# Two transformer layers on one core: three edits to layer norms and weight copies at the seams of a TensorE-bound kernel

## The chip, the core and the metric

The kernel runs on one core of a Trainium2 chip. A core has five engines with instruction streams of their own: TensorE (PE, matrix products), VectorE (DVE), ScalarE (ACT), GpSimd (POOL) and SyncE (SP, which here only issues transfers), and 16 DMA engines that all queues share. The metric is the device time of one launch in microseconds (us), lower is better. A time is the median of several runs; the profile describes one further run.

## The reference

The input x has 2048 tokens of 512 features, in fp32. There are 32 heads of 16 features, and a hidden layer of 1792.

```python
def _layernorm(x, axis=-1, eps=1e-5):
    m = jnp.mean(x, axis=axis, keepdims=True)
    v = jnp.var(x, axis=axis, keepdims=True)
    return (x - m) / jnp.sqrt(v + eps)

def _A_ref(x, wqkv, wo):            # q, k, v = x @ wqkv, 32 heads of 16
    scores = jnp.einsum("bhqd,bhkd->bhqk", q, k) * (Dh ** -0.5)
    p = _softmax(scores, axis=-1)
    o = jnp.einsum("bhqk,bhkd->bhqd", p, v)
    return o.reshape(B, S, D) @ wo

def _B_ref(x, w1, b1, w2):          # Dense, Mish, Dense
    h = x @ w1 + b1
    sp = jnp.log1p(jnp.exp(-jnp.abs(h))) + jnp.where(h > 0, h, 0)
    return (h * jnp.tanh(sp)) @ w2

x = A_x
x = x + _A_ref(_layernorm(x), A_wqkv, A_wo)
x = x + _B_ref(_layernorm(x), B_w1, B_b1, B_w2)
x = x + _A_ref(_layernorm(x), A_wqkv, A_wo)
x = x + _B_ref(_layernorm(x), B_w1, B_b1, B_w2)
```

Both layers use the same weights.

## The kernel before

**Precision.** TensorE works on fp32r operands, a shorter form of fp32. Each fp32 operand is therefore split into a high part (a rounded copy) and a low part (the operand less its high part), and a product takes three matmuls: high x high, high x low, low x high (`mm3`, L196). What PE computes in PSUM is split on the way out by `split_psum` (L192): ACT writes the high part, then DVE the low part.

**Stages.** The 2048 tokens go in four chunks of 512 (`NCH`); a chunk has four token tiles of 128 tokens. Per layer: a layer norm of each chunk gives `th` and `tl`, the high and low parts of the normed chunk turned over (features on the partitions); `qkv` makes the projections of Q and K, each a tile `qk` of 128 features x 512 tokens in PSUM, emptied into a `pt` tile and stored to DRAM (`scr<-pt`), from where `ks` and `qs` are gathered by heads; then come the V phase, the attention, the output projection with residual, a second norm and the hidden layer with residual.

**Order.** PE's order is written down by hand: each matmul is chained to the one before (`att.pe`). `behind` pins the order of other instructions to the order of the program text; what isn't pinned is placed by the framework's scheduler, which decides by its own estimate of time before the kernel is built. Tiles come from pools of a fixed number of buffers (`blk`: 22 large ones; `tmp` with the tags `raw`, 3 buffers, and `f` and `ah`, 2 each); a new tile waits for the last reader of the tile whose buffer it takes.

**The first norm** (`norm_parts` with the tag `mx`) makes statistics of a token tile on DVE (`bn_stats`, `bn_aggr`), the reciprocal root on POOL (`rstd`, L209), and the scaled tile `xn` on DVE (L218). PE then transposes two token tiles into one PSUM tile `tp` of two banks (L248), and one `split_psum` empties both. Between these steps PE runs a few matmuls on a tile of zeros (`warm_up`). The first two weights, `sqkv0` and `sqkv2`, are loaded and split beside it by `split_load`: the high part on ACT (L153), the low part (L156) on DVE for `sqkv0` and on POOL for `sqkv2`.

**The V phase** (`v_parts`) makes the projection of V. For every two token tiles POOL clears a tile `v` (L628), PE makes the product, ACT empties it into `v` (L642), and SP stores it to DRAM (`vscr<-v`, L646). Twelve of the sixteen token tiles are done at the end of `qkv`, the last chunk inside the attention's start.

**The weights kept.** Layer 1 uses the split weights of layer 0 again. `keep` (L142) copies a split weight to DRAM by a DMA of POOL's queue. The six of QKV are copied by `keep_all` at attention step 3, after the last clearing of `v`.

**Layer 1's last norm** (`norm_units(..., wide=True)`, `late` in the layer loop) works on the last chunk of layer 0's output, which is ready last. It is a sequence of steps that `qkv` takes between its projections: four of statistics, four of scaling plus a 32x32 block transpose on DVE (`xn` to `y`), stores of `y` to DRAM (`ntq<-yq`, L308, two sets of four on SP's queue), a load back in turned order (L317), and the rounding (L320, L321). The list in the layer loop says ahead of which projection each step stands:

```python
order = [(0, 0), (0, 1), (4, 0), (4, 1), (1, 0), (0, 2), (4, 2), (1, 1), (1, 2), (5, 0), ...]
for n in (0, 0, 0, 0, 1, 1, 2, 2, 2, 9, 10):
    within.setdefault((n, 0), []).append(lambda: next(late))
```

A pair in `order` is (block of 128 features, chunk). Every second projection (even number) puts its `pt` into the `raw` ring, the others into `blk` buffers.

Of the kernel before, what the change touches and what calls it, by code (L numbers as in the profile page):

```python
# [9 lines left out]
F32 = mybir.dt.float32  # L10
# [8 lines left out]
P = 128  # L19
# [21 lines left out]
AHEAD = 21  # L41
PRE = 3
KEEP = 3
PREP = 2
WARM = (4, 1, 1)
GSTEPS = NCH * NKT
# [32 lines left out]
def kernel(ctx: ExitStack, tc: tile.TileContext, x, wqkv, wo, w1, b1, w2, out):  # L79
# [25 lines left out]
    def b8(shape, dt, name):  # L105
        return blk.tile(shape, dt, tag="blk", name=name)
# [21 lines left out]
    def behind(ins):  # L128
        return tc.keep_in_program_order(ins)
# [73 lines left out]
    def norm_parts(src, nm, got, key, tag, fine=False, pin=lambda ins: ins, pe=lambda ins: ins, halves=False):  # L203
        st = tmp.tile([P, NCH, 6], F32, tag="st", name=f"st{nm}")
        mv = tmp.tile([P, NCH, 2], F32, tag="mv", name=f"mv{nm}")
        ve = tmp.tile([P, NCH], F32, tag="ve", name=f"ve{nm}")
        rs = tmp.tile([P, NCH], F32, tag="rs", name=f"rs{nm}")

        def rstd(t, n):  # L209
            nc.gpsimd.tensor_scalar(ve[:, t : t + n], mv[:, t : t + n, 1], EPS, None, op0=ALU.add)  # L210
            nc.gpsimd.tensor_tensor(rs[:, t : t + n], ve[:, t : t + n], mhalf[:, t : t + n], op=ALU.pow)

        xns = []

        def scaled(t, tag):
            xn = t512(tag, f"xn{nm}{t}")
            pin(
                nc.vector.tensor_scalar(  # L218
                    xn, src[:, t], mv[:, t, 0:1], rs[:, t : t + 1], op0=ALU.subtract, op1=ALU.mult
                )  # L220
            )
            return xn

        def next_scaled():
            xns.append(scaled(len(xns), ("f", "ah")[len(xns) // 2]))

        for t in range(NCH):
            pin(nc.vector.bn_stats(st[:, t], src[:, t]))
            pin(nc.vector.bn_aggr(mv[:, t], st[:, t]))
            if fine:  # L230
                rstd(t, 1)
                if t and tag == "mx":
                    next_scaled()
        if not fine:
            rstd(0, NCH)
        yield
        th = b8([P, KT, CW], F32R, f"th{nm}")
        tl = b8([P, KT, CW], F32R, f"tl{nm}")
        got[key] = (th, tl)
        if tag == "mx":  # L240
            while len(xns) < NCH:
                next_scaled()
            yield
            for u in range(NCH // 2):
                tp = ps.tile([P, 2, 512], F32, tag=tag, name=f"tp{nm}{u}")
                for e in range(2):
                    for k in range(KT):
                        pe(nc.tensor.transpose(tp[:, e, ts(k, P)], xns[2 * u + e][:, ts(k, P)], ident))  # L248
                two = ts(u, 2 * P)
                split_psum(  # L250
                    th[:, :, two].rearrange("p k (t n) -> p k t n", n=P),
                    tl[:, :, two].rearrange("p k (t n) -> p k t n", n=P),
                    tp.rearrange("p t (k n) -> p k t n", n=P),
                    pin,
                )
                yield
            return
        for t in range(NCH):
            xn = scaled(t, "f")
            if halves:  # L260
                yield
            tp = pbank(tag, f"tp{nm}{t}")
            for k in range(KT):
                pe(nc.tensor.transpose(tp[:, ts(k, P)], xn[:, ts(k, P)], ident))
            split_psum(th[:, :, ts(t, P)], tl[:, :, ts(t, P)], tp.rearrange("p (k n) -> p k n", k=KT), pin)
            yield
# [7 lines left out]
    def norm_units(src, nm, got, key, wide=False):  # L274

        st = tmp.tile([P, NCH, 6], F32, tag="st", name=f"st{nm}")
        mv = tmp.tile([P, NCH, 2], F32, tag="mv", name=f"mv{nm}")
        ve = tmp.tile([P, NCH], F32, tag="ve", name=f"ve{nm}")
        rs = tmp.tile([P, NCH], F32, tag="rs", name=f"rs{nm}")
        for t in range(NCH):  # L280
            behind(nc.vector.bn_stats(st[:, t], src[:, t]))
            behind(nc.vector.bn_aggr(mv[:, t], st[:, t]))
            if t == NCH - 1:
                nc.gpsimd.tensor_scalar(ve, mv[:, :, 1], EPS, None, op0=ALU.add)
                nc.gpsimd.tensor_tensor(rs, ve, mhalf, op=ALU.pow)
            yield
        turned = dram.tile([D, CW], F32, name=f"nt{nm}")
        for h in range(2):
            if wide and h == 0:
                xns = b8([P, 2, 2, D], F32, f"xn{nm}")  # L290
                ys = b8([P, 2, D // TR, 2, TR], F32, f"y{nm}")
            if wide:
                xn, y = xns[:, h], ys[:, h]
            else:
                xn = tmp.tile([P, 2, D], F32, tag="raw", name=f"xn{nm}{h}", bufs=3)
                y = tmp.tile([P, D // TR, 2, TR], F32, tag="raw", name=f"y{nm}{h}", bufs=3)
            for j in range(2):
                t = h + 2 * j
                behind(
                    nc.vector.tensor_scalar(  # L300
                        xn[:, j], src[:, t], mv[:, t, 0:1], rs[:, t : t + 1], op0=ALU.subtract, op1=ALU.mult
                    )
                )
                behind(nc.vector.transpose(y[:, :, j], xn[:, j].rearrange("p (b r) -> p b r", r=TR)))
                if j:
                    for a in range(P // TR):
                        n0 = h * CW // 2 + a * 2 * TR
                        nc.sync.dma_start(  # L308
                            turned[:, n0 : n0 + 2 * TR].rearrange("(b q) n -> q b n", q=TR),
                            y[ts(a, TR)].rearrange("q b j r -> q b (j r)"),  # L310
                        )
                yield
        th = b8([P, KT, CW], F32R, f"th{nm}")
        tl = b8([P, KT, CW], F32R, f"tl{nm}")
        got[key] = (th, tl)
        raw = tl.bitcast(F32)
        nc.sync.dma_start(raw, turned.rearrange("(k p) n -> p k n", p=P))  # L317
        yield
        for k in range(KT):
            behind(nc.scalar.activation(th[:, k], raw[:, k], AF.Copy))  # L320
            behind(nc.vector.tensor_tensor(tl[:, k], raw[:, k], th[:, k].bitcast(F32), op=ALU.subtract))  # L321
            if k % 2:
                yield
# [6 lines left out]
    class Attention:  # L330
# [10 lines left out]
        def pe(self, ins):  # L341
            if self.chained:
                if self.last is not None:
                    follow(ins, self.last)
                self.last = ins
# [213 lines left out]
    def qkv(l, att, wts, tt, order, within, due):  # L559
# [57 lines left out]
        for c in range(NCH - 1):  # L617
            for _ in v_parts(l, c, wts, tt, att, False):
                i += 1
                if i % 3 == 0:  # L620
                    some_max()

# [197 lines left out]
            keep(*unkept.pop(0))  # L820

    xc = [load_x(0)]
    load_qkv(0, wts, (0,), splits, nc.vector)
    load_qkv(0, wts, (2,), splits)
    xc += [load_x(c) for c in range(1, NCH)]
    nc.sync.dma_start(b1t, b1.rearrange("(f p) -> p f", p=P))
    att = attention(0)
    att.chained = True
    norms = [norm_parts(xc[c], f"q0{c}", tt, c, "mx", True, behind, att.pe) for c in range(NCH)]
    warm = b8([P, CW], F32, "warm")  # L830
    nc.vector.memset(warm, 0.0)

# [4 lines left out]

    warm_up(0, WARM[0])
    next(norms[0])
    splits.pop(0)()  # L840
    next(norms[0])
    next(norms[0])
    warm_up(1, WARM[1])
    splits.pop(0)()
    next(norms[0])
# [2 lines left out]
    for l in range(2):  # L848
        due, within = {}, {}
        if l == 0:  # L850
            order = [(m, c) for c in range(NCH) for m in (0, 4, 1, 5)[: (4, 4, 3, 2)[c]]]
            due[4, 0] = [lambda: load_qkv(0, wts, (1, 3), splits)]
            due[4, 2] = [lambda: load_qkv(0, wts, (4, 5), later)]
            due[0, 3] = [lambda: split_all(splits)]
            due[5, 2] = [lambda: split_all(later)]
            for c, spots in enumerate((((0, 0), (0, 0), (2, 2), (3, 1)), ((3, 2), (3, 2), (6, 1), (6, 3)), ((6, 3), (6, 3), (9, 1), (9, 3))), 1):
                for at in spots:
                    within.setdefault(at, []).append(lambda c=c: next(norms[c]))
        else:
            order = [(0, 0), (0, 1), (4, 0), (4, 1), (1, 0), (0, 2), (4, 2), (1, 1), (1, 2), (5, 0), (5, 1), (5, 2), (0, 3), (4, 3)]  # L860
            att = attention(1)
            att.chained = True
            late = norm_units(x2s[NCH - 1], f"q1{NCH - 1}", tt, NCH - 1, True)
            for n in (0, 0, 0, 0, 1, 1, 2, 2, 2, 9, 10):
                within.setdefault((n, 0), []).append(lambda: next(late))
        order += [(m, c) for m in (1, 5, 2, 6, 3, 7) for c in range(NCH) if (m, c) not in order]
        qkv(l, att, wts, tt, order, within, due)
# [133 lines left out]
```

## Time and profile before

| what | value |
|---|---|
| median of 3 runs | 3491.2 us (3490.45 to 3491.69) |
| profiled execution, its own time | 3490.85 us |
| its span, first to last instruction | 3489.1 us |
| PE busy | 3475.0 us |
| DVE, ACT, POOL busy | 3004.8, 2576.3, 238.0 us |
| mean granted TensorE clock | 1.000 |

Rows of a timeline show the start, the duration, the engine, the line of the kernel, the operation, what it writes and reads, and how many instructions were put together; in brackets stands the idle time of the engine before it and what ended that. Names are those of the kernel's tiles with numbers left out (`thq`, `tlq`, `xnq` are `th`, `tl`, `xn` of the QKV norms). PE's rows with `x4` are matmuls in a row; their times overlap, since matmuls are pipelined. `SPq`, `POOLq` and `ACTq` are the engines' queues that issue transfers; their duration is that of issuing, not of the transfer.

### The profile page before, as it was taken

To read this page: it belongs to the slowest core of one execution; us is meant where nothing else is said; L and a number is where in the kernel's file an instruction comes from. 1 tells how busy PE (TensorE), PEld (TensorE's weight loads), DVE (VectorE), ACT (ScalarE), POOL (GpSimd) and SP (SyncE) were. 2 spreads that over 40 slices of the span, in tenths; PEclk is the share of its full clock that TensorE was granted. 3 is DMA by queue.
4 is the path that set the end of the run, shared out by engine and by line. 5 is a ranking of instruction groups with operands and counts; after the bars stand their busy time and mean duration, and the time that the engine had idled before them with its cause. 6 is when DMAs were issued, how large, how long until landed. Compare 5 with 4: busy or idle time off the path is not lost.

```text
span 3489.1 us, 68659 instructions
## 1 busy us (share of the span) xinstructions
PE 3475.0 (100%) x28556; PEld 1923.1 (55%) x28556; DVE 3004.8 (86%) x3178; ACT 2576.3 (74%) x3517; POOL 238.0 (7%) x384
## 2 busy tenths in 40 slices
PE   9999999999999999999999999999999999999999
PEld 7644444444444444888876444444444444448887
DVE  6699999999999996767756999999999999957675
ACT  3288888888888889456622888888888888884565
POOL 3100010001001002100010000000000000021000
PEclk9999999999999999999999999999999999999999
DMA  7741313222131314722375202111120212156210
GB/s 246 234 93 43 64 60 75 50 53 72 51 63 56 65 36 96 229 67 73 109 242 158 45 21 58 32 38 34 33 48 21 50 29 48 21 114 213 76 37 25
DMA packets 190019, 277.09 MB, mean 79 GB/s; under 512 B 76356, under 2 KB 118276, under 8 KB 175884
## 3 DMA queue, kind: packets, MB, share of 16 engines
q1 hardware_dynamic: 162788, 196.05, 22.8%
q10 hardware_dynamic: 19176, 43.06, 3.6%
q0 software_dynamic: 7744, 33.60, 3.3%
q8 instruction: 224, 3.67, 0.5%
q14 instruction: 87, 0.71, 0.1%
HBM read 159.92 MB, written 111.67 MB: 78 GB/s over the span
## 4 chain that ended last, share of the span: by engine, by line
PE 97%; DVE 1%; ACT 1%; issue 0%; DMA 0%; POOL 0%; DVEq 0%; SPq 0%; ACTq 0%; POOLq 0%
PE pv L484 30%; PE pm L406 18%; PE ss L468 13%; PE sp L458 9%; PE h L747 9%; PE mo L773 8%; PE qk L199 2%; PE qk L200 1%; PE qk L201 1%; PE wo L199 1%; PE wo L201 1%; PE wo L200 1%; PE va L199 1%; PE va L201 1%; PE va L200 1%
## 5 line engine op out<-in xcount | busy, mean ns | idle before, releaser
L410 DVE TENSOR_REDUCE mxv<-pm 128x2 f32<-128x1024 f32 x2048 | 2385.6, 1219 | 144.6 <-PE pm L406 93.9
L459 ACT ACTIVATE p<-sp 128x1024 f32<-128x1024 f32 x1366 | 1395.6, 1022 | 6.6 <-PE ss L468 1.3
L484 PE MATMUL pv<-p,va 128*32 128x256 f32 (+2 forms) x16032 | 1165.7, 392 | 0.5 <-ACT ot L508 0.5
L406 PE MATMUL pm<-ks,qs 48*128 48x512 f32 x4096 | 1101.2, 447 | 0.5
L469 ACT ACTIVATE p<-ss 128x512 f32<-128x512 f32 x1364 | 814.6, 597 | 332.1 <-PE ss L468 255.0
L458 PE MATMUL sp<-qs,ks 50*128 50x512 f32 x2732 | 737.8, 444 | 1.1 <-ACT p L459 1.1
L484 PEld LDWEIGHTS pv<-p,va 128*32 128x32 f32 x16032 | 368.9, 109 | 502.2 <-issue 423.1
L406 PEld LDWEIGHTS pm<-ks,qs 48*128 48x128 f32 x4096 | 453.3, 184 | 346.1 <-issue 186.3
L468 PE MATMUL ss<-qs,ks 50*128 50x512 f32 x1364 | 611.4, 448 | 0.5 <-ACT v L642 0.5
L468 PEld LDWEIGHTS ss<-qs,ks 50*128 50x128 f32 x1364 | 252.4, 185 | 325.8 <-ACT p L469 234.7
L458 PEld LDWEIGHTS sp<-qs,ks 50*128 50x128 f32 x2732 | 268.1, 183 | 186.2 <-ACT p L459 109.1
L427 POOL CAST hi<-nt 128x32 fp32r<-128x32 f32 x64 | 13.3, 208 | 2246.7 <-DVE nt L423 2246.7
L750 ACT ACTIVATE hb<-h,b1t 128x512 f32<-128x512 f32 x112 | 77.1, 689 | 100.0 <-PE h L747 99.2
L754 ACT ACTIVATE hr<-he 128x512 f32<-128x512 f32 x112 | 70.8, 632 | 104.7 <-DVE he L753 104.0
L193 ACT ACTIVATE pt<-qk 128x512 fp32r<-128x512 f32 x64 | 37.8, 596 | 140.9 <-PE qk L201 107.2
L751 DVE TENSOR_SCALAR he<-hb 128x512 f32<-128x512 f32 x112 | 47.6, 425 | 80.5 <-ACT hb L750 74.5
L757 DVE TENSOR_TENSOR hb<-hb,hr 128x512 f32<-128x512 f32 x112 | 77.5, 692 | 45.0 <-ACT hr L755 42.9
L761 DVE TENSOR_TENSOR al<-hb,ah 128x512 fp32r<-128x512 f32 x112 | 77.4, 691 | 28.8 <-ACT ah L760 23.1
L760 ACT ACTIVATE ah<-hb 128x512 fp32r<-128x512 f32 x112 | 70.2, 627 | 29.9 <-DVE hb L757 29.9
L753 DVE SCALAR_TENSOR_TENSOR he<-he 128x512 f32<-128x512 f32 x112 | 76.8, 685 | 17.2 <-ACT he L752 17.2
L755 ACT ACTIVATE hr<-hr,lnhalf 128x512 f32<-128x512 f32 x112 | 81.1, 724 | 3.6
L752 ACT ACTIVATE he<-he 128x512 f32<-128x512 f32 x112 | 70.4, 629 | 17.9 <-DVE he L751 17.9
(224 smaller groups left out, 2976.7 us busy)
## 6 DMA issues: line engine op xcount, KB each, us to landing
scr<-pt ACTq DMA_DIRECT2D x64, 512.0 KB
qs<-scr SPq DMA_DIRECT2D x174, 128.0 KB
ks<-scr SPq DMA_DIRECT2D x174, 128.0 KB
vscr<-v SPq DMA_DIRECT2D x32, 512.0 KB
va<-vscr SPq DMA_DIRECT2D x64, 256.0 KB
oscr<-ot SPq DMA_DIRECT2D x64, 256.0 KB
ww<-sw POOLq DMA_DIRECT2D x14, 1024.0 KB, 4.3
num<-oscr SPq DMA_DIRECT2D x64, 128.0 KB
```

The source lines that it names most:

```text
L199: pe(nc.tensor.matmul(acc, ah, bh, start=first and i == 0, stop=False))
L200: pe(nc.tensor.matmul(acc, ah, bl, start=False, stop=False))
L201: pe(nc.tensor.matmul(acc, al, bh, start=False, stop=last and i == n - 1))
L406: nc.tensor.matmul(pm[:, e], qs[u][rows, q0 : q0 + P], ks[u][rows, ts(n, 512)], start=True, stop=True)
L410: nc.vector.tensor_reduce(self.mxs[b][:, 2 * u : 2 * u + 2, qt, n], pm, axis=AX.X, op=ALU.max)
L458: self.pe(nc.tensor.matmul(sp[:, e], k, q, start=True, stop=True))
L459: nc.scalar.activation(self.pts[-1][:, 0:n], sp[:, 0:n], AF.Exp, scale=SCALE)
L468: self.pe(nc.tensor.matmul(sp, k, q, start=True, stop=True))
L469: nc.scalar.activation(self.pts[i // 3][:, 2], sp, AF.Exp, scale=SCALE)
L484: nc.tensor.matmul(self.accs[b][ts(h, VW), cols], self.va[b // NCH][:, kt, h, :], self.pts[j][:, e, cols], start=kt == 0 and q0 == 0, stop ...
L747: pe(nc.tensor.matmul(acc, w[:, part, k, ts(f % 2, P)], t[:, k, :], start=i == 0, stop=i == 3 * KT - 1))
L773: nc.tensor.matmul(obs[c][t // 2][:, t % 2], act[:, ts(t, P)], w[:, part, f % 2], start=f == part == 0 and act is ah, stop=f == FT - 1 and ...
```

## The change

Three edits.

A, the start. For the first chunk, each token tile is split by itself as soon as PE has transposed it (four ACT and four DVE instructions on 128x512 in place of two each on 128x1024), still in one PSUM tile for two. For all four chunks, the first scaled tile comes after the second tile's statistics, the second and third after the fourth's. The low part of `sqkv0` moves from DVE to POOL, and the weights' splits go one step later in ACT's order.

B, the V phase of layer 0. Four of the six QKV weights are copied to DRAM at four steps of the V phase; the last two stay where all six were.

C, layer 1's last norm. `xn` lies in `tmp` tiles of tags `f` and `ah`, `y` in the `raw` ring, which takes two `blk` buffers less; and its steps are spread over more projections.

```diff
+KEPT = (4, 12, 20, 28)
@@ norm_parts
             if fine:
                 rstd(t, 1)
-                if t and tag == "mx":
+                for _ in range((0, 1, 0, 2)[t]):
                     next_scaled()
@@
                 for e in range(2):
+                    t = 2 * u + e
                     for k in range(KT):
-                        pe(nc.tensor.transpose(tp[:, e, ts(k, P)], xns[2 * u + e][:, ts(k, P)], ident))
+                        pe(nc.tensor.transpose(tp[:, e, ts(k, P)], xns[t][:, ts(k, P)], ident))
+                    if halves:
+                        split_psum(
+                            th[:, :, ts(t, P)], tl[:, :, ts(t, P)], tp[:, e].rearrange("p (k n) -> p k n", n=P), pin
+                        )
+                if halves:
+                    yield
+                    continue
@@ norm_units
-            if wide and h == 0:
-                xns = b8([P, 2, 2, D], F32, f"xn{nm}")
-                ys = b8([P, 2, D // TR, 2, TR], F32, f"y{nm}")
             if wide:
-                xn, y = xns[:, h], ys[:, h]
+                xn = [t512(("f", "ah")[h], f"xn{nm}{h}{j}") for j in range(2)]
             else:
-                xn = tmp.tile([P, 2, D], F32, tag="raw", name=f"xn{nm}{h}", bufs=3)
-                y = tmp.tile([P, D // TR, 2, TR], F32, tag="raw", name=f"y{nm}{h}", bufs=3)
+                pair = tmp.tile([P, 2, D], F32, tag="raw", name=f"xn{nm}{h}", bufs=3)
+                xn = [pair[:, j] for j in range(2)]
+            y = tmp.tile([P, D // TR, 2, TR], F32, tag="raw", name=f"y{nm}{h}", bufs=3)
@@ qkv, V phase
             for _ in v_parts(l, c, wts, tt, att, False):
                 i += 1
+                if l == 0 and i in KEPT:
+                    keep(*unkept.pop(0))
@@ start
-    load_qkv(0, wts, (0,), splits, nc.vector)
-    load_qkv(0, wts, (2,), splits)
+    load_qkv(0, wts, (0, 2), splits)
...
-    norms = [norm_parts(xc[c], f"q0{c}", tt, c, "mx", True, behind, att.pe) for c in range(NCH)]
+    norms = [norm_parts(xc[c], f"q0{c}", tt, c, "mx", True, behind, att.pe, c == 0) for c in range(NCH)]
...
     next(norms[0])
-    splits.pop(0)()
     next(norms[0])
     next(norms[0])
+    splits.pop(0)()
     warm_up(1, WARM[1])
@@ layer loop
-            for n in (0, 0, 0, 0, 1, 1, 2, 2, 2, 9, 10):
+            for n in (0, 0, 1, 1, 2, 2, 3, 4, 5, 9, 10):
                 within.setdefault((n, 0), []).append(lambda: next(late))
```

More of the change, by code (lines that the diff above doesn't have):

```diff
@@ L300, in norm_units @@
                     nc.vector.tensor_scalar(
-                        xn[:, j], src[:, t], mv[:, t, 0:1], rs[:, t : t + 1], op0=ALU.subtract, op1=ALU.mult
+                        xn[j], src[:, t], mv[:, t, 0:1], rs[:, t : t + 1], op0=ALU.subtract, op1=ALU.mult
                     )
                 )
-                behind(nc.vector.transpose(y[:, :, j], xn[:, j].rearrange("p (b r) -> p b r", r=TR)))
+                behind(nc.vector.transpose(y[:, :, j], xn[j].rearrange("p (b r) -> p b r", r=TR)))
                 if j:
```

## Prediction, made before the changed kernel was run

> **What bounds the kernel now.** The page was read first: the engines' shares, then the chain that ended last.
>
> ```profile
> span 3489.1 us, 68659 instructions
> ...
> PE 3475.0 (100%) x28556; PEld 1923.1 (55%) x28556; DVE 3004.8 (86%) x3178; ACT 2576.3 (74%) x3517; POOL 238.0 (7%) x384
> ...
> PE 97%; DVE 1%; ACT 1%; issue 0%; DMA 0%; POOL 0%; DVEq 0%; SPq 0%; ACTq 0%; POOLq 0%
> ```
>
> TensorE is busy for 3475.0 of 3489.1 us, and 97% of the last chain is its own matmuls. The change leaves its list of matmuls as it is, in number and order. So the most that any edit could bring is the 14.1 us in which PE isn't busy, and the time moves only by how long PE stands still near the three edited places. The second view is PE's list of waits (total us, times, longest):
>
> ```profile
> PE qk L199 <- DVE pt L194: 2.9, 2, 1.4
> ...
> PE sp L458 <- ACT p L459: 1.1, 1, 1.1
> PE tpq L248 <- DVE xnq L218: 1.0, 3, 0.7
> ```
>
> These are the three places: the two waits of the projections are at layer 1's last norm, the one of `sp` stands right behind the V phase of layer 0, and the `tpq` waits lie in the first norm. The profiled execution took 3490.85 us, 1.75 outside its span and 0.35 under the median of 3491.2; I sum against 3490.85 and add 0.35 at the end.
>
> **Part A, the start.** Timeline of the first 27 us, by engine (start, duration, engine, line, operation; in brackets the idle time before it and what ended it). PE:
>
> ```profile
> 6.83 0.60 PE L248 MATMUL tpq<-ident,xnq 128*128 128x128 f32 x4
> ...
> 8.10 1.02 PE L836 MATMUL warm<-warm 128*128 128x512 f32 x2
> ...
> 12.00 2.21 PE L589 MATMUL qk<-thq,sqkv 128*128 128x512 f32 x8 [0.25 <-ACT thq L193]
> ...
> 15.18 1.07 PE L589 MATMUL qk<-thq,sqkv 128*128 128x512 f32 x4
> ...
> 17.00 1.07 PE L589 MATMUL qk<-thq,sqkv 128*128 128x512 f32 x4
> ...
> 26.02 0.50 PE L200 MATMUL qk<-tlq,sqkv 128*128 128x512 f32 x1 [0.49 <-DVE tlq L194]
> ```
>
> DVE, ACT and POOL:
>
> ```profile
> 9.63 0.54 DVE L218 TENSOR_SCALAR xnq<-x,mvq,rsq 128x512 f32<-128x512 f32 x1 [0.76 <-POOL rsq L211]
> 10.61 1.23 DVE L194 TENSOR_TENSOR tlq<-tpq,thq 128x1024 fp32r<-128x1024 f32 x1 [0.43 <-ACT thq L193]
> ...
> 16.01 0.69 DVE L194 TENSOR_TENSOR pt<-qk,pt 128x512 fp32r<-128x512 f32 x1 [0.31 <-ACT pt L193]
> ```
>
> ```profile
> 8.60 1.06 ACT L153 ACTIVATE sqkv<-rqkv 128x1024 fp32r<-128x1024 f32 x1 [6.60 <-DMA rqkv<-in_A_wqkv_dram]
> ...
> 15.38 0.60 ACT L193 ACTIVATE pt<-qk 128x512 fp32r<-128x512 f32 x1 [2.49 <-PE qk L589]
> ```
>
> ```profile
> 12.97 2.39 POOL L156 TENSOR_TENSOR sqkv<-rqkv,sqkv 128x1024 fp32r<-128x1024 f32 x1 [3.38 <-ACT sqkv L153]
> ```
>
> Before, PE turns two token tiles into one PSUM tile of two banks, ACT writes the high part of both at once and DVE the low part of both at once. Afterwards each token tile is rounded by itself, but both still lie in the same PSUM tile, and the built program lets PE's transposes of the second token tile wait for DVE's low part of the first. So what ran side by side becomes a chain: transpose, high, low, next transpose. And DVE's order is fixed: the low part of tile 0 stands behind all four scalings, the last of which waited for POOL's `rsq` at 9.63 in the row above.
>
> Lay it out with these rows. The last scaling ended at 9.63 + 0.54 = 10.17; in the new order the statistics of the last tile come up to 0.5 earlier (one scaling of about that length no longer stands before them), but POOL needs its time, so I take 9.9. Low part of tile 0: 0.69 (the 128x512 row at 16.01), to 10.6. Transposes of tile 1: 0.60, to 11.2. High part of tile 1 on ACT: 0.60 (row at 15.38), to 11.85 with the hand-over. ACT then does the high part of the weights, 1.06, to 12.9; meanwhile PE does its warm-up (two rows, 1.02) and the transposes of tile 2. High part of tile 2 to 13.5, low to 14.2, transposes of tile 3 to 14.8, its high part to 15.4. The first projection starts there, at 15.45 in place of 12.00. It is then shorter: it had pauses inside (12.00 to 15.18 until the next projection starts, 3.18), and now runs through in 12 x (17.00 − 15.18)/8 = 2.73. The second projection starts at 18.2 in place of 15.18: +3.0.
>
> Of that a part comes back, since what waits for DVE later has had more time: the 0.49 at 26.02. Against it stand the following chunks' statistics, which now end before their second scaling and deliver that later, taken as 0.3, half of one DVE pass over 128x512 (0.69). The weights' low part that leaves DVE for POOL (2.39 there) ends at 12.9 + 2.4 = 15.3, just before PE needs it at 15.45 + 0.9, and costs nothing; if ACT were a microsecond later, it would cost that microsecond. Part A: +3.0 − 0.5 + 0.3 = **+2.8**, between +2.0 (more comes back) and +3.5 (nothing does, and each of eight hand-overs is 0.05 longer).
>
> **Part B, four weights kept in the V phase.** The issue queues, SP and POOL, and what DMA moved (windows: length, busy time of the five engines, granted clock, DMA share, GB/s):
>
> ```profile
> 152.36 18.93 SPq L646 DMA_DIRECT2D vscr<-v  x4
> ```
>
> ```profile
> 153.52 3.21 POOL L144 DMA_DIRECT2D wqkv<-sqkv  x6
> ```
>
> ```profile
> 80.00:100.00 20.00, 20.00 (x90) 13.73 (x91) 16.31 (x17) 3.59 (x6) 3.37 (x2) 1.00 0.73 211
> 100.00:125.00 25.00, 24.89 (x111) 16.70 (x109) 20.75 (x21) 3.97 (x7) 3.62 (x2) 1.00 0.64 215
> ...
> 150.00:175.00 25.00, 24.60 (x105) 17.50 (x104) 3.90 (x4) 9.33 (x14) 4.97 (x7) 1.00 0.97 358
> ```
>
> PE behind it, in layer 0 and at the same places of layer 1, which keeps no weights:
>
> ```profile
> 181.82 0.85 PE L484 MATMUL pv<-p,va 128*32 128x384 f32 x8
> ...
> 184.43 0.50 PE L458 MATMUL sp<-qs,ks 50*128 50x512 f32 x2 [1.08 <-ACT p L459]
> ```
>
> ```profile
> 1398.99 0.50 PE L199 MATMUL wo<-wo0l,oh 128*128 128x512 f32 x1
> ```
>
> ```profile
> 1916.81 0.85 PE L484 MATMUL pv<-p,va 128*32 128x384 f32 x8
> ```
>
> ```profile
> 3133.10 0.50 PE L199 MATMUL wo<-wo0l,oh 128*128 128x512 f32 x1
> ```
>
> Six copies of 1 MB are issued together at 153.52 and fill the DMA engines (0.97 busy, 358 GB/s) while SP stores V; its four stores there take 18.93 us to issue. ACT's exponentials write to a buffer that such a store must free, and PE loses 1.08 at 184.43. Is this loss recovered later in the attention? From the `pv` at 181.82 to the output projection at 1398.99 are 1217.17 us; in layer 1, 1916.81 to 3133.10 are 1216.29. Layer 0 is 0.88 longer, so most of the 1.08 stays. With two copies left behind the last memset, a third of the backlog is there, and the stall should go: **−1.0**, at best −1.4 (the 0.4 that PE lacks in the window of 150 to 175), at worst 0 (the store waits for something else).
>
> The four moved copies now run beside the gathers of K and Q, between about 80 and 125. At 369 GB/s (358 / 0.97) one takes 2.84 us of all the engines, four 11.4; the free share there is 20 x 0.27 + 25 x 0.36 = 14.4 us. They fit, spaced by some 14 us each. I count nothing for it; where the cover is gone, the rival below has the price. POOL issues each behind a memset that it did anyway, and the next memset is ten microseconds away.
>
> The Trainium skill (DMA: Bandwidth & Descriptors, Queues, rings and completion order) says that a DMA engine takes turns between the queues that have work, packet by packet. By that a lone copy would slow a gather and not stop it, which leaves the sum at nothing too; the row at 152.36 neither proves nor contradicts it.
>
> **Part C, layer 1's last norm.** PE and DVE, then SP's queue:
>
> ```profile
> 1765.48 0.50 PE L199 MATMUL qk<-thq,qkv0l 128*128 128x512 f32 x1 [1.45 <-DVE pt L194]
> ...
> 1778.08 0.50 PE L199 MATMUL qk<-thq,qkv2l 128*128 128x512 f32 x1 [1.41 <-DVE pt L194]
> ```
>
> ```profile
> 1763.10 0.55 DVE L300 TENSOR_SCALAR xnq<-x,mvq,rsq 128x512 f32<-128x512 f32 x1 [1.47 <-POOL rsq L285]
> ...
> 1764.74 0.68 DVE L194 TENSOR_TENSOR pt<-qk,pt 128x512 fp32r<-128x512 f32 x1
> ```
>
> ```profile
> 1729.63 2.13 SPq L308 DMA_DIRECT2D ntq<-yq  x4
> 1733.81 0.38 SPq L317 DMA_DIRECT2D tlq<-ntq  x1
> ...
> 1767.12 6.45 SPq L308 DMA_DIRECT2D ntq<-yq  x8
> ```
>
> At 1765.48 PE needs a PSUM bank that DVE empties with the `pt` of 1764.74; DVE did this late, behind norm steps that waited 1.47 for POOL. In the new order this emptying stands before the norm, and the stall goes, with a small pause behind it: −1.6. The second stall (1.41) hangs on the emptying of a later projection: it stays or goes with what follows. What the change adds: `y` now lies in the ring of three `raw` buffers that the projections' `pt` tiles also use. So the `pt` of the seventh projection must wait until all four `ntq<-yq` stores of the first half have landed. The quiet case: four stores and the load that waits for them are issued from 1729.63 to 1733.81, so the stores had landed 4.2 us after the first issue. Eight stores beside other traffic took 6.45 merely to issue. The first half of `y` is ready at about 1765.7; ACT and DVE then need 0.60 + 0.69 and 0.1 of hand-over, and the ninth projection wants its bank at about 1772.1 (three projections of 2.73 behind 1765.48 less 1.6). With 4.2 the bank is free at 1771.3, and nothing is lost; with 6.5 at 1773.6, and 1.5 is lost. Queued behind that wait is ACT's order: the later `pt` and the late rounding. Part C lies between −1.8 and +0.8 (the first loss comes back entirely and one more wait is late by 0.8); I take the middle, nearer to the quiet row, **−0.9**.
>
> **The sum.** +2.8 − 1.0 − 0.9 = +0.9 on 3490.85 gives 3491.75, as a median 3492.1.
>
> **The rivals.** *The first norm costs little*: DVE's low part of tile 0 finds its place between the scalings, and the chain hides behind the loads. Then A is +0.5, with B and C −1.9, in all −1.4: 3489.8. For it speaks that the tiles' parts are half as long; against it, that DVE's order is fixed. Chance 0.13.
>
> *The late norm waits*: the stores take the busy latency, C is +0.8, the total +2.6: 3493.8. For it: eight stores in 6.45. Against it: they are now spread over more projections. Chance 0.2.
>
> *The clock falls* (slower). The new chain leaves PE idle from about 7.4 to 10.6, where the longest wait of the first norm is 0.7 now (the list of waits). What a cold PE costs shows in the warm-up tile (durations min/median/max in ns):
>
> ```profile
> L836 PE MATMUL warm<-warm x12: 592/596/1219, 1.4 to 11.2; 128*128 128x512 f32 x12
> ```
>
> The first ones take 1219, the later ones 592. The Trainium skill (TensorE: Matmul & The Clock Gate, Part 1: The HAM clock gate) says that PE goes back to half its clock after an idle window of about 3.4 us. The trace shows no idle time of that length after the start; 1.45 did not do it. From the rows: if 3.2 us of idle time decides it, the transposes (3 x 0.6), one warm-up pair (0.5 of it on the path) and some 6 to 10 projection matmuls at 0.23 double, +3.5; with the rest +4.4: 3495.6. Below an idle time of about three microseconds it doesn't occur. Chance 0.14.
>
> *The copies hold up the gathers* (slower by most). If each of the four stops the gathers for its 2.84 and PE has no slack there, up to 11.4 less what is covered, some +7 to +12: from 3498. Against it: 20.00 of 20.00 and 24.89 of 25.00 busy in these windows, with DMA at 0.73 and 0.64. It decides once the gathers' slack is under about 3 us. Chance 0.08.
>
> **How the numbers follow.** My forecast has the remaining 0.45, with 3490.0 to 3494.0 as its own range. A measurement of this kernel can tell about 0.2%, 7.0 us, from no change; nearly all cases lie within it. Slower by more: the copies, and a little for a longer cold stretch, 0.11. Faster by more would need half of all of PE's idle time: 0.03. Within: 0.86. The range from 3488.5 to 3496.5 leaves out the copies and the tails of both sides.
>
> **What would show it.** Right: the first projection (`qk`, two sets of eight) starts at about 15.4, with transposes that wait for DVE `tlq`; `wqkv<-sqkv` in five or so separate rows on POOL from 80 on, and no wait of `sp` on ACT near 184; no wait at the sixth projection near 1765. Wrong: a first projection before 13; a PE clock under 1 behind 10; `ks` or `qs` waits between 80 and 125; a median outside the range.

## The result: slower by 6 us, and the profile after

The changed kernel took 3497.6 us (median of 18 runs, 3495.41 to 3499.45), the kernel before 3491.3 (15 runs beside them, 3490.43 to 3492.92). The ratio is 1.0017, 95% interval 1.001 to 1.0025: 6 us slower. The forecast was 3492.1 with a range to 3496.5, so it missed by 5.5 us, on the slow side; within 0.2%, which had 0.86, it is only just. All medians are over the runs whose granted clock was near full speed (0.997 or more where it is on record, at least 5 runs of a kernel); the other runs, some 20 us and more longer, are all of kernels without part B's edit, the kernel before among them (three of its 18 here), and the profiled run of the second kernel with a changed order is one of them.

The profiled execution took 3497.56, 6.7 us more than that of before. The page of the changed kernel, and its list of waits of PE (total, times, longest):

```profile
span 3495.7 us, 68666 instructions
...
PE 3476.4 (99%) x28556; PEld 1921.6 (55%) x28556; DVE 3002.9 (86%) x3179; ACT 2576.6 (74%) x3519; POOL 239.3 (7%) x385
```

```profile
PE qk L200 <- DVE pt L195: 5.1, 2, 3.7
PE tpq L250 <- DVE tlq L195: 4.1, 2, 2.6
...
PE sp L465 <- ACT v L651: 0.7, 1, 0.7
```

PE has the same 28556 matmuls. The wait of `sp` on ACT's `p` is gone, the transposes now wait 4.1 for DVE, and the projections wait 5.1 in place of 2.9, once 3.7 at a stretch.

Where the time changed is read from PE's timeline: since PE's order is unchanged, any matmul can be laid beside itself. The changed kernel at the places that the prediction shows of before, and one more:

```profile
29.32 0.50 PE L201 MATMUL qk<-tlq,sqkv 128*128 128x512 f32 x1 [0.47 <-DVE tlq L195]
```

```profile
1401.00 0.50 PE L200 MATMUL wo<-wo0l,oh 128*128 128x512 f32 x1
```

```profile
1778.72 0.50 PE L200 MATMUL qk<-thq,qkv2l 128*128 128x512 f32 x1 [1.41 <-DVE pt L195]
...
1790.85 0.50 PE L200 MATMUL qk<-thq,qkv0l 128*128 128x512 f32 x1 [3.67 <-DVE pt L195]
...
1795.29 0.40 PE L200 MATMUL qk<-thq,qkv2l 128*128 128x512 f32 x1
```

```profile
3139.20 0.50 PE L200 MATMUL wo<-wo0l,oh 128*128 128x512 f32 x1
```

and the thirteenth and fourteenth projection in the kernel before:

```profile
1786.37 0.40 PE L199 MATMUL qk<-thq,qkv0l 128*128 128x512 f32 x1
...
1789.32 0.39 PE L199 MATMUL qk<-thq,qkv2l 128*128 128x512 f32 x1
```

| place | before | after | how much later |
|---|---|---|---|
| first chunk's end (26 us) | 26.02 | 29.32 | +3.30 |
| output projection, layer 0 | 1398.99 | 1401.00 | +2.01 |
| tenth projection, layer 1 | 1778.08 | 1778.72 | +0.64 |
| thirteenth projection, layer 1 | 1786.37 | 1790.85 | +4.48 |
| fourteenth projection, layer 1 | 1789.32 | 1795.29 | +5.97 |
| output projection, layer 1 | 3133.10 | 3139.20 | +6.10 |
| end of the span | 3489.1 | 3495.7 | +6.6 |

The start costs 3.3, the V phase brings 1.3 back, the first half of the late norm another 1.4; then 5.3 are lost between the tenth and the fourteenth projection. The last 0.5 lie in layer 1's hidden stage, which the change doesn't touch. Two single executions can differ by up to 0.9 where nothing was changed: with the list of steps alone, whose start is that of before, the matmul of 26.02 stands at 26.88, with part B alone at 26.33.

**The start.** PE's timeline:

```profile
7.29 0.60 PE L250 MATMUL tpq<-ident,xnq 128*128 128x128 f32 x4
10.45 0.66 PE L250 MATMUL tpq<-ident,xnq 128*128 128x128 f32 x4 [2.56 <-DVE tlq L195]
...
13.96 0.66 PE L250 MATMUL tpq<-ident,xnq 128*128 128x128 f32 x4 [1.55 <-DVE tlq L195]
...
15.30 2.10 PE L596 MATMUL qk<-thq,sqkv 128*128 128x512 f32 x8
...
18.14 1.07 PE L596 MATMUL qk<-thq,sqkv 128*128 128x512 f32 x4
```

This is the chain of the prediction, within 0.15: first projection at 15.30 (forecast 15.45), second at 18.14 (18.2).

**The V phase.** POOL's issues now stand one by one, from 84.68 to 141.81 (the last two):

```profile
84.68 0.59 POOL L145 DMA_DIRECT2D wqkv<-sqkv  x1
...
141.81 1.10 POOL L145 DMA_DIRECT2D wqkv<-sqkv  x2
```

**The late norm.** ACT and SP, then the windows of that stretch (length, the five engines' busy time, granted clock, DMA share, GB/s):

```profile
1772.92 0.60 ACT L194 ACTIVATE pt<-qk 128x512 fp32r<-128x512 f32 x1 [2.46 <-DMA ntq<-yq]
...
1778.70 1.96 ACTq L608 DMA_DIRECT2D scr<-pt  x3
1788.24 1.15 ACT L327 ACTIVATE thq<-tlq 128x512 fp32r<-128x512 f32 x2 [9.32 <-DMA scr<-pt]
1789.30 1.06 ACT L194 ACTIVATE pt<-qk 128x512 fp32r<-128x512 f32 x2
```

```profile
1768.49 5.95 SPq L315 DMA_DIRECT2D ntq<-yq  x8
1779.18 0.38 SPq L324 DMA_DIRECT2D tlq<-ntq  x1
```

```profile
1790.00:1791.00 1.00, 0.15 (x1) 0.15 (x2) 1.00 (x3) 0.36 (x1) 0.00 (x0) 1.00 0.02 5
1791.00:1792.00 1.00, 1.00 (x4) 0.76 (x5) 0.49 (x2) 0.76 (x2) 0.00 (x0) 0.65 0.28 109
1792.00:1793.00 1.00, 1.00 (x4) 0.80 (x3) 1.00 (x2) 0.88 (x2) 0.00 (x0) 0.50 1.03 397
1793.00:1794.00 1.00, 1.00 (x3) 0.78 (x3) 0.80 (x2) 0.00 (x0) 0.00 (x0) 0.50 1.06 406
1794.00:1795.00 1.00, 1.00 (x4) 0.79 (x3) 0.00 (x0) 0.00 (x0) 0.00 (x0) 0.65 0.71 258
```

Read from the bottom: PE's wait of 3.67 at 1790.85 is for a bank that DVE empties behind the rounding. In ACT's order the rounding (`thq`, 1788.24) stands before the `pt` that empties this bank (1789.30), and it waits for the load that SP issued at 1779.18, 9 us earlier. The bracket at 1788.24 names a store, `scr<-pt`; that it is the load shows in SP's queue, whose own wait for it ends in the same moment, ahead of its row at 1788.20 (SP's list of waits):

```profile
SPq L370 <- DMA tlq<-ntq: 8.6, 1, 8.6
```

The thirteenth projection also reads this norm's data, so with the bank free it would still have stood until about 1788.9, the end of the first `thq` (an estimate: 1788.24 and about 0.6): about 1.7 of the 3.67. The wait for `ntq<-yq` at 1772.92 is the ring of `raw` buffers. After PE's pause the granted clock falls to 0.50 for about three and a half microseconds. Two losses, then, by the table: the pause (from +0.64 to +4.48), and the half clock behind it (from +4.48 to +5.97).

### The profile page after: what moved, and what is told of

Same layout as the page of the kernel before. It is cut to its first block, busy times and chain, and to the rows that moved or that the text cites. A ratio compares the mean times of both kernels' runs of the same rounds, so it can differ in the third digit from the quotient of the medians.

```text
span 3495.7 us, 68666 instructions
## 1 busy us (share of the span) xinstructions
PE 3476.4 (99%) x28556; PEld 1921.6 (55%) x28556; DVE 3002.9 (86%) x3179; ACT 2576.6 (74%) x3519; POOL 239.3 (7%) x385
## 3 DMA queue, kind: packets, MB, share of 16 engines
q8 instruction: 224, 3.67, 0.5%
## 4 chain that ended last, share of the span: by engine, by line
PE 96%; DVE 1%; DMA 1%; ACT 1%; issue 0%; POOL 0%; SPq 0%; DVEq 0%; ACTq 0%; POOLq 0%
PE pv L491 30%; PE pm L413 18%; PE ss L475 13%; PE sp L465 9%; PE h L756 8%; PE mo L782 8%; PE qk L200 1%; PE qk L202 1%; PE qk L201 1%; PE wo L200 1%; PE wo L202 1%; PE wo L201 1%; PE va L200 1%; PE va L202 1%; PE va L201 1%; DVE mxv L417 0%
## 5 line engine op out<-in xcount | busy, mean ns | idle before, releaser
L195 DVE TENSOR_TENSOR pt<-qk,pt 128x512 fp32r<-128x512 f32 x64 | 43.6, 685 | 50.0 <-ACT pt L194 49.9
```

## The experiments

Kernels that were timed together shared the runs of the kernel before; its median over the runs counted was 3491.1 in the first four, 3491.6 in the others.

### The three parts, each alone

Part A alone (the edits of `norm_parts`, of `load_qkv` and of the first `splits`):

> Part A alone. Theory: the four transposes of the first norm became a chain through DVE's low parts; the chain costs what the traces show in the first 20 us (3.0 to 3.3 us) and all of it stays: 3491.2 + 3.1 = 3494.3, first projection at about 15.3. Rival: the start is partly recovered later, before the attention is full, and the rest of the difference is one of noise between runs: +1 to +2.

Measured: 3493.5, +2.4 against before; first projection at 15.08. At first the chain costs what it was said to cost, 3.1 (15.08 against 12.00). Not all of it stays: at the end of the profiled span 2.0 of it are left (3491.1 against 3489.1). So the result lies between the theory and its rival, and where the rest comes back is open.

Part B alone:

```diff
+                if l == 0 and i in KEPT:
+                    keep(*unkept.pop(0))
```

> Part B alone. Theory: the wait of sp on ACT behind the V phase goes, and nothing takes its place: -1.1 to -1.3 us against before, no waits for ks or qs between 80 and 125. Rival: the wait went in the changed kernel only because the whole start was 3 us later there; then 0.

Measured: 3490.6, −0.5, less than the theory said, and the runs overlap (3490.03 to 3491.07 against 3490.2 to 3494.0). In the profile PE reaches layer 0's output projection at 1397.86 in place of 1398.99, 1.1 earlier, no wait of `sp` on `p` is left, and none for `ks` or `qs` came; by the medians it is half of that. The wait is gone in the trace; in the time the gain is small.

Part C alone (the edits of `norm_units` and the list of steps):

> Part C alone. Theory: y in the ring of pt tiles holds the pt stores back, these meet the second half of the norm's stores and its load, which lands about 9 us after its issue, and the thirteenth projection waits: +3 to +4.5 us against before. Rival: the load fell behind the stores only because parts A and B had shifted the traffic; then C alone is near the forecast, -1.8 to 0.

Measured: 3496.3, +5.2, more than the theory said. So the loss doesn't hang on A and B having shifted the traffic. The profiled run was the quickest of the eight counted (3493.07), so its trace shows the loss at its mildest; what it was in the runs near the median has no trace. It had a pause of PE of 2.33 at the thirteenth projection, and the clock fell behind it as well (windows of this kernel):

```profile
1786.00:1788.00 2.00, 0.27 (x1) 0.27 (x2) 2.00 (x4) 1.25 (x3) 0.00 (x0) 1.00 0.21 75
1788.00:1790.00 2.00, 2.00 (x7) 1.52 (x7) 1.49 (x4) 1.64 (x3) 0.00 (x0) 0.60 0.72 280
```

### Inside part C: the steps or the buffers

Only the list of steps, on the buffers of before:

```diff
-            for n in (0, 0, 0, 0, 1, 1, 2, 2, 2, 9, 10):
+            for n in (0, 0, 1, 1, 2, 2, 3, 4, 5, 9, 10):
```

> Only the list of steps of part C, with xn and y in their two large buffers as before. Theory (the ring of y is at fault): no projection waits for the norm's stores, the first stall goes, the load lands as before or earlier: -1 to -3 us. Rival (the later place of the steps is at fault, above all the load at projection 5 in place of 2): the thirteenth projection waits about as in the changed kernel, +2 to +4.

Only the buffers, on the steps of before:

```diff
-                xns = b8([P, 2, 2, D], F32, f"xn{nm}")
-                ys = b8([P, 2, D // TR, 2, TR], F32, f"y{nm}")
+                xn = [t512(("f", "ah")[h], f"xn{nm}{h}{j}") for j in range(2)]
...
+            y = tmp.tile([P, D // TR, 2, TR], F32, tag="raw", name=f"y{nm}{h}", bufs=3)
```

> Only the buffers of part C, with the list of steps as before. Theory (the ring of y is at fault): pt tiles wait for the norm's stores, the scr stores come later and meet the load, which lands 8 us or more after its issue; the thirteenth projection waits 2 to 4 us: +2 to +4 against before. Rival (the two together are needed): the load is issued early enough, no such wait, -1.5 to +0.5.

Measured: the steps alone 3489.9, −1.2; the buffers alone 3497.0, +5.4, more than the theory said. The steps are not at fault, the buffers are. PE in the run with the steps alone, then in that with the buffers alone:

```profile
1787.52 0.50 PE L199 MATMUL qk<-thq,qkv0l 128*128 128x512 f32 x1 [0.21 <-ACT thq L320]
```

```profile
1790.71 0.79 PE L199 MATMUL qk<-thq,qkv0l 128*128 128x512 f32 x1 [3.85 <-DVE pt L194]
```

Both rows lie in the thirteenth projection. With the steps alone it starts at 1785.79 without a wait, and stands 0.21 within, for the rounded data; with the buffers alone it waits 3.85 for its bank before it starts. Between the two lies when SP's load is issued, and beside what:

```profile
1776.84 0.38 SPq L317 DMA_DIRECT2D tlq<-ntq  x1
```

```profile
1780.01 0.38 SPq L315 DMA_DIRECT2D tlq<-ntq  x1
```

With the steps alone the load goes out ahead of the stores that ACT issues next, with the buffers just behind the first of three (ACT's issues at 1777.46 and 1779.99). From its issue to the rounding on ACT passed 6.9 us in the one (`thq` at 1783.76) and 8.1 in the other (1788.09). That the stores are what slows the load is the likeliest reading. The transfers on record fit it: between the load's issue and the rounding 0.47 MB of stores moved beside its 1.05 MB in the kernel before (6.5 us), 1.54 MB in the changed one (9.1 us). No run took the stores away, so it is not shown.

The two runs differ in one more thing. With the steps alone the scheduler put one `pt` more ahead of the rounding on ACT (1783.26, `thq` at 1783.76), and the thirteenth projection found its bank free; with the buffers alone that bank is emptied behind the rounding (1789.15), as in the kernel before (1784.65) and in the changed one (1789.30). So the clean pair is the buffers alone and the kernel before, with the same steps and the same order there: the load is issued at 1780.01 in place of 1777.06, the rounding starts at 1788.09 in place of 1783.60, and the projection at 1790.71 in place of 1786.37. That order may also help the steps alone; no run parts the two.

Not all that the profile of the buffers alone lost is the late norm's. Behind the V phase of layer 0, which this edit doesn't touch, `sp` waited 1.34, as it does in the kernel before (1.08), and here the clock fell behind it (windows). PE was 0.54 later than before at the start of that and 1.96 at its end:

```profile
182.61:186.03 3.42, 2.08 (x23) 0.75 (x15) 2.22 (x3) 2.03 (x3) 0.00 (x0) 1.00 1.08 327
186.03:189.44 3.41, 3.41 (x29) 1.43 (x21) 2.17 (x2) 2.10 (x3) 0.00 (x0) 0.50 0.31 73
```

### What PE waits for

Part C with projections of other chunks put ahead of the last chunk's two:

```diff
-            order = [..., (5, 2), (0, 3), (4, 3)]
+            order = [..., (5, 2), (2, 0), (2, 1), (0, 3), (4, 3)]
```

> Part C with two projections of chunks 0 and 1 put ahead of the two of the last chunk; the steps of the norm stay ahead of projections 9 and 10. Theory (PE waits for its bank, whose emptying stands behind the rounding on ACT and DVE): the wait is still at the thirteenth projection although that doesn't use the late norm, 2 us and more, and the time is about that of part C alone, +3 to +5. Rival (PE waits for the normed data): the wait is gone or moves two projections on with 5.5 us less, -2 to -1 in all.

The same, and the list's last steps at 11 and 12 in place of 9 and 10:

> As the run before, and the two rounding steps two projections later as well. Both theories of the wait expect it gone, as long as the load lands within 5.5 us more than its 9: -1.5 to -2.5 against before, granted clock 1.00 throughout that stretch. If a wait of over 1 us stays there, the late load isn't the whole cause.

Measured: 3509.2 (+17.6) and 3501.7 (+10.1). As a mend both failed, for a reason not thought of: the gathers for the first group of heads start only when the fourth chunk's projections are done (SP's first `qs<-scr` at 1802.18 in the first, 1796.53 with part C alone), and the row maxima (`pm`) wait for them. As tests of the wait they speak. The first of the two (its list of waits, and PE's row at the thirteenth projection):

```profile
PE pm L404 <- DMA scr<-pt: 4.7, 1, 4.7
```

```profile
1787.94 0.50 PE L199 MATMUL qk<-thq,qkv1l 128*128 128x512 f32 x1 [1.94 <-DVE pt L194]
```

That projection reads `thq` of chunk 0 and waits all the same: it waits for the bank. With the rounding two projections later there is no wait of over 1.41 left among the projections, as expected. The rest of both is in the stops of `pm`, 7.8 in the profile of the first (4.7, 2.1 and 1.0) and 7.3 in that of the second, and in half clock behind them; a window of the first, behind the 4.7, with 12 matmuls in 5 us where the full clock has 24:

```profile
1855.00:1860.00 5.00, 5.00 (x12) 3.49 (x11) 1.73 (x2) 0.00 (x0) 0.00 (x0) 0.50 0.02 3
```

### The pause and the half clock

The changed kernel, with matmuls that work while PE would wait:

```diff
+            if l and n == 12:
+                spare_bank = ps.tile([P, 2, 512], F32, tag="mx", name="fill")
+                for _ in range(12):
+                    att.pe(nc.tensor.matmul(spare_bank[:, 0], w[:, 0, 0, 0:P], tt[0][0][:, 0], start=True, stop=True))
```

> The changed kernel with twelve matmuls (2.73 us warm, result unused) ahead of the thirteenth projection, so that PE works through most of its pause of 3.67. Theory (the pause costs itself and also a stretch at half clock behind it, which the windows of the changed kernel show as 0.50): clock 1.00 behind the pause, and about 1.7 us faster than the changed kernel, 3495.9. Rival (the slow matmuls behind the pause have another cause, the DMA traffic of that stretch): the matmuls are slow all the same, and the time is that of the changed kernel, 3497.6.

Measured: 3495.4, 2.2 less than the changed kernel's 3497.6. PE and the windows in that run:

```profile
1787.25 2.88 PE L594 MATMUL fill<-thq,qkv0l 128*128 128x512 f32 x12
1790.94 0.50 PE L200 MATMUL qk<-thq,qkv0l 128*128 128x512 f32 x1 [0.81 <-DVE pt L195]
...
1794.00 0.39 PE L200 MATMUL qk<-thq,qkv2l 128*128 128x512 f32 x1
```

```profile
1791.00:1792.00 1.00, 1.00 (x5) 0.81 (x6) 0.49 (x2) 0.67 (x2) 0.00 (x0) 1.00 0.19 74
1792.00:1793.00 1.00, 1.00 (x5) 0.63 (x4) 1.00 (x2) 0.97 (x2) 0.00 (x0) 1.00 1.04 399
```

The projection starts as late as before (1790.94 against 1790.85), twelve matmuls more are run, and the kernel is faster: the clock stays at 1.00 beside the same DMA traffic (399 GB/s against 397). So the half clock has the pause as its cause. In the traces it costs 1.4: from the thirteenth to the fourteenth projection pass 4.44 us in the changed kernel, 3.06 here. Of the 2.2 between the two profiled spans another 0.45 lie at the start, which this edit doesn't touch (first projection at 14.85 against 15.30).

### The start mended, and the best of both

Part A with the second tile of each pair in a bank of its own:

```diff
+                        one = ps.tile([P, 2, 512], F32, tag=tag, name=f"tp{nm}{t}")[:, 0] if e == 0 else pbank("s", f"tp{nm}{t}")
```

> Part A alone, but the second token tile of each pair is transposed into a PSUM bank of its own (one of the three that the projections use). Theory (the shared PSUM tile makes the chain): PE's transposes no longer wait for DVE's low part, the first projection starts at about 12.2 and the second at about 15.3; -0.5 to +0.5 against before, in place of about +2 for part A. Rival (DVE's order, with the low parts behind all four scalings, is enough to hold the start): first projection at 14 or later, +1.5 to +2.5.

Measured: 3490.9, −0.7; first projection at 11.75. PE's timeline:

```profile
9.84 1.04 PE L250 MATMUL tpq<-ident,xnq 128*128 128x128 f32 x8
...
13.24 1.20 PE L600 MATMUL qk<-thq,sqkv 128*128 128x512 f32 x4 [0.30 <-POOL sqkv L156]
...
15.19 1.07 PE L600 MATMUL qk<-thq,sqkv 128*128 128x512 f32 x4
```

The transposes run without a wait, and the second projection starts at 15.19 (before: 15.18). DVE's first low part still stands behind the scalings (9.66, with part A alone 9.50), so its order isn't what holds the start: the shared PSUM tile alone makes the chain. The second projection is no earlier than in the kernel before; PE now stands 0.30 for the weights' low part on POOL.

Part A with warm-up matmuls in its pauses (`warm_up(t + 2, 2 if t == 1 else 1)` ahead of the transposes of tiles 1 and 3):

> Part A alone with three more warm-up matmuls in the two pauses of its start (1.7 us in the first, 0.9 in the second). In the runs of part A alone four of nine undisturbed ones had a granted clock of 0.999 and were 2.4 us longer than the others. Theory (in those the pause let the clock fall): all undisturbed runs at 1.000 and one group, 3493.0 to 3493.6. Rival (those four had another cause): two groups as before, a few at 0.999 with some 2 us more.

Measured: 3493.5, and one of ten runs at 0.999 in place of four of nine. It points to the theory, but six of 24 runs of the kernel before beside part A were at 0.999 too, and the clock can fall elsewhere, as at 186.03 with the buffers alone; so it is not settled.

Part B and the list of steps, on the buffers and the start of before; and all three parts with both mends:

> Part B and the list of steps of part C, on the buffers and the start of before. Both gains were seen alone; theory: they add up, -1.3 for the wait behind the V phase and -1.0 to -1.8 for the first projection wait less what the late norm still costs at the thirteenth projection: 3488.5 to 3489.5, 2 to 2.7 under before. Rival: the load lands late again by chance of the transfers, and then 3490 to 3492.

> All three parts, with the two mends: tiles of the first norm in PSUM banks of their own, the late norm's xn and y in their large buffers. Theory: the sum of the two runs before it, within 0.5 of the run with parts B and C's list alone: 3488.5 to 3490. Rival: the first norm's banks come out of the ring of the projections and hold up the first of them: 1 us or more above that run.

Measured: 3489.35 and 3489.4 (medians of 12 runs), −2.2 and −2.1 against 3491.55. All twelve runs of the first (3488.49 to 3490.0) and ten of the second are below the lowest of the 21 of the kernel before, 3490.52. The two gains add up. Both kernels beat before and after; the mended start adds nothing to the other two.

## Why the prediction was wrong, point by point

- **Part A**, forecast +2.8: +3.30 in the trace, +2.4 by the runs. The chain's steps were right to 0.3 us each. The 0.5 that was to come back there didn't: the wait at 26.02 is there at 29.32 too, 0.47 in place of 0.49, because everything ahead of it moved together. With part A alone about 1 us came back later (3.1 at the first projection, 2.0 at the end); what brought it back is open.
- **Part B**, forecast −1.0: −1.29 in the trace, −0.5 by the runs alone. Right in the mechanism and, in the trace, in size. The copies did not collide with the gathers.
- **Part C**, forecast −0.9 between −1.8 and +0.8: +4.0 in the trace (from +2.01 to +5.97), +5.2 alone. This is the step that failed. "The stall goes, −1.6" was right, and so was the second stall, 1.41 in both. The wait on the `raw` ring is there too, at 1772.92, and was all but covered. But the sum ended at the ninth projection. What stands behind the wait was named ("the later `pt` and the late rounding") and not priced: the stores go out later, the load later still, the rounding comes 4.64 later (1788.24 against 1783.60), and the bank of the thirteenth projection is emptied behind it. In the trace of before that projection came through with next to no slack, and the prediction has no row of it: the two `pt` below end at about 1786.1 and 1786.7, and PE used the first one's bank at 1786.37 (ACT, then DVE, of the kernel before). So nearly all of the delay counted, +3.84 from the tenth projection to the thirteenth, and the half clock behind the pause added 1.49; the prediction had that only as a rival at the start. By the prediction's own rows the busy stores give −1.6 + 1.5 = −0.1; the bound of +0.8 adds the return of the first stall and 0.8 more, and had no row behind it that reached this far.

```profile
1783.60 1.15 ACT L320 ACTIVATE thq<-tlq 128x512 fp32r<-128x512 f32 x2 [5.31 <-DMA tlq<-ntq]
```

```profile
1785.47 1.28 DVE L194 TENSOR_TENSOR pt<-qk,pt 128x512 fp32r<-128x512 f32 x2
```

- **The late norm waits**, with 0.2: it named the ring of `raw` buffers, and that wait is there, but it was all but covered: the ninth projection starts at 1774.30 with no wait shown. The loss came four projections later, through the queue behind the ring; so both the wait and the size (+2.6 in all, in place of 6) were wrong.
- **The clock falls**, with 0.14: the mechanism came true, but at the late norm and not at the start, where the pause of 2.56 left the clock at 1.00 in the profiled run (its windows from 7.5 to 15). Its threshold, "about three microseconds", was wrong: a pause of 2.33 was enough in the run of part C alone, one of 1.94 in that with the changed order (0.50 from 1788.42 to 1791.84), and 1.34 with the buffers alone, though the prediction says that 1.45 did not do it in the kernel before. The Trainium skill (TensorE: Matmul & The Clock Gate, Part 1: The HAM clock gate) has a window of about 3.4 us that runs freely; the length of the slow stretch, 0.50 from 1791.29 to 1794.71 in the changed kernel, agrees with that, and the pauses suggest that it matters where in such a window a pause falls (figures in the last section). A pause of the full length it didn't take. Its price was too high for what came: 3 x 0.6 + 0.5 + 6 to 10 x 0.23 gives 3.7 to 4.6 (the prediction says 3.5), and the half clock at the late norm cost 1.4 to 1.5.
- **The copies hold up the gathers**: not seen.

In the sum: 2.8 − 1.0 − 0.9 was forecast, 3.3 − 1.3 + 4.0 came, and 0.6 in places that the change doesn't touch.

## What to carry to other kernels

When a step on a side engine gets a new wait, follow it through the queue behind it until something has slack that you can show in a row, and not just to the next use. A ring shared by two streams ties their release times together: here the norm's stores held back the projections' buffers, and no run shows a gain from the freed large buffers. Where PE would have to pause for a few microseconds, useless matmuls in the pause can be cheaper than the half clock behind it; and a tile that is to be worked on by halves must lie in two allocations, or the halves wait for each other.

## What was not expected of the hardware

A pause of PE of 2.33 us, with PE busy for 0.27 of 2.00 in that window, was followed by a granted clock of 0.60 and 0.50; one of 2.56 at the start of the changed kernel was not. By the clock records of these traces the granted clock changes at times that lie whole multiples of 3.413 us apart (in the first with a changed order 3.41, 27.31, 3.41, 30.72 and 6.83). Laid out in such steps the two pauses differ: the one of 2.33 lies within one step, the one of 2.56 is cut in two. The windows of part C alone, then of the changed kernel, whose clock record begins at 6.12:

```profile
1784.98:1788.39 3.41, 1.08 (x5) 0.56 (x4) 2.49 (x4) 2.39 (x5) 0.00 (x0) 1.00 0.43 163
1788.39:1791.80 3.41, 3.41 (x10) 2.64 (x9) 1.89 (x3) 1.37 (x3) 0.00 (x0) 0.50 0.88 333
```

```profile
6.12:9.54 3.42, 1.77 (x7) 0.76 (x6) 2.91 (x7) 0.60 (x1) 1.92 (x5) 1.00 0.98 337
9.54:12.95 3.41, 1.96 (x10) 1.19 (x10) 1.55 (x3) 1.80 (x3) 0.18 (x1) 1.00 1.03 398
```

PE was busy for 1.08 of 3.41 in the step ahead of the fall, for 1.77 and 1.96 in the two that had none. That share is not the whole of it, since with the buffers alone the clock fell behind a step with 2.08; what decides there is open. Twelve matmuls of 2.88 us more, put into the pause, made the kernel 2.2 us shorter.
